# Expert stage: next slot's second unit and two weight pieces moved behind the second layer's first block

## The chip, the cores and the metric

The kernel runs on one core of a Trainium2 chip. The metric is device time in microseconds (us) of one execution, median of the runs. A core has five engines that run side by side: TensorE (PE in the profile; PEld is its loading of stationary operands), VectorE (DVE), ScalarE (ACT), GpSimd (POOL) and SyncE (SP). Semaphores order them. Each engine takes its instructions in the order in which the program issues them.

## The reference

Three parts follow each other, all in float32:

```python
x = attention(q, k, v)                 # 8 x 8 heads, 576 positions, blocks of 64
x = ((x @ w1) * (x @ w2) @ w3) @ w_out # 4608 tokens, 512 -> 1024 -> 512
# mixture of 8 experts, one expert for each token
logits = x @ w_gate                    # (4608, 8)
expert = argmax(logits); gate = softmax(logits)[expert]
for e in range(8):
    out[expert == e] = gate * (relu(x[expert == e] @ e1[e]) @ e2[e])   # 512 -> 1024 -> 512
```

The change touches only the last loop.

## The kernel before

The experts' work is cut into slots. A slot belongs to one expert and holds one unit of 128 token rows (a single) or two (a pair). The order is planned at build time: 17 pairs, with four singles put between them, after the 3rd, 6th, 10th and 13th pair. More singles can follow under a run-time condition; in this run none does. The expert of a slot is known at run time only. GpSimd gathers its weight tables by index: `wload(2 * s)` brings the first layer's table of slot s (128 partitions x 4096 numbers) into raw buffer 0, `wload(2 * s + 1)` the second layer's into raw buffer 1. If the expert is that of the slot before, the index lies out of bounds, and nothing is fetched.

Every matrix product is done in three matmuls, of high and low parts: a float32 operand is split into a rounded high part and the rest. `wsplit(i, c)` splits piece c (1024 of the 4096 columns) of table i: ScalarE copies the high part at L725, and the low part is a subtraction at L727, on GpSimd for piece 1 and on VectorE for the pieces 0, 2 and 3. Three sets of split tables (`wset`) rotate.

`xprep(s, parts)` prepares the rows of a slot: `tr8` transposes each unit by four TensorE transposes (L775) into one of three PSUM scratch buffers, ScalarE copies the high part (L777) and VectorE subtracts for the low part (L778). The buffer is free again after that.

`run` goes through the slots in order: `l1(s)`, then the preparation of the next slot, then `l2(s)`. Nothing reorders the instructions afterwards; what is written between two groups of matmuls is what each engine does between them. `hook1` and `hook2` are called at set points of the two layers and do work for later slots:

- `hook1(0)`: gather the rows of slot s + 2 and split pieces 0 and 1 of table 2s + 2 (the next slot's first layer).
- `hook1(1)`: split pieces 2 and 3 of it, and gather table 2s + 4 into the raw buffer that is free then (the first layer two slots on).
- `hook1(2)`: scatter the last finished output unit to memory.
- `hook2(0)`, `hook2(1)`: split the four pieces of table 2s + 3 (the next slot's second layer), then gather table 2s + 5.

In a pair, `l1` works with the weights as stationary operand, in four parts `f2` of 24 matmuls, each followed by a relu (L832), a subtraction (L833) and a hook. Part f2 needs piece f2 of the split table. In a single, the rows are stationary (L847): two halves of 12 matmuls, each with a relu into `hr` (L850). The hidden rows must then be transposed: `turn(0)` and `turn(1)` do so for each half with `tr8`, which ends in the two halves of `hh` (high) and `hw` (low). The order of a single's `l1` is: first half, relu, `hook(0)` and `hook(1)`, second half, relu, `turn(0)`, the next slot's first unit (`xprep(s + 1, (0,))`), `turn(1)`, `hook(2)`. In `run`, the next slot's second unit follows (`xprep(s + 1, (1,))`).

`l2` sums eight blocks g of three matmuls (L872) for each unit. In block g the first two matmuls read `hh[:, g]`, the third `hw[:, g]`; blocks 0 to 3 need only what `turn(0)` wrote. Behind blocks 1 and 3 come `hook2(0)` and `hook2(1)`. At the end ScalarE scales and copies the output (L878).

Of the kernel before, what the change touches and what calls it, by code (L numbers as in the profile page):

```python
# [31 lines left out]
def slot_order(nt):  # L32

    npr, nsg = slots(nt)
    now = min(nsg, 4)
    order = []
    for j in range(npr):
        order.append((True, j))
        for m in range(now):
            if j == (m + 1) * npr // (now + 1) - 1:  # L40
                order.append((False, m))
    order += [(False, m) for m in range(nsg) if (False, m) not in order]
    return order, npr + now
# [3 lines left out]
def tile_moe_stack(ctx: ExitStack, tc: tile.TileContext, qd, kd, vd, w1, w2, w3t, wo, wg,  # L47
# [10 lines left out]
    order, NOW = slot_order(NT)  # L58
# [671 lines left out]
    def units(s):  # L730
        pair, j = order[s]
        return (s, NSL + j) if pair else (s,)
# [7 lines left out]
    def experts(sc):  # L740
# [9 lines left out]
        def scatter():  # L750
            if ys:
                un, y = ys.pop(0)
                nc.gpsimd.indirect_dma_start(  # L753
                    out=out, out_offset=bass.IndirectOffsetOnAxis(ap=ids[:, un:un + 1], axis=0),
                    in_=y[:], in_offset=None, bounds_check=NT - 1, oob_is_err=False)
# [8 lines left out]
        def rload(s):  # L764
            rows[s] = []
            for h in range(len(units(s))):
                x = gx.tile([128, RW], F32, tag=f"x{h}", name=f"x{h}")
                rgather(s, h, 1, x[:])
                rows[s].append(x)

        def tr8(src, dh, dl):
            for h, (s_, o_) in enumerate(src):
                ps = ps_t.tile([128, 512], F32, tag="t", name="t")
                for c in range(4):
                    nc.tensor.transpose(ps[:, 128 * c:128 * c + 128], s_[:, 128 * c:128 * c + 128], ident)  # L775
                ps = ps.rearrange("p (k c) -> p k c", c=128)
                nc.scalar.activation(out=o_(dh), in_=ps, func=AF.Copy)  # L777
                nc.vector.tensor_tensor(out=o_(dl), in0=ps, in1=o_(dh).bitcast(F32), op=ALU.subtract)  # L778

        def xprep(s, parts=(0, 1)):  # L780
            o_ = 256 * (s % 2)
            xh, xl = xhl[:, 0:4, o_:o_ + 256], xhl[:, 4:8, o_:o_ + 256]
            tr8([(x, lambda t, h=h: t[:, :, 128 * h:128 * h + 128]) for h, x in enumerate(rows[s]) if h in parts], xh, xl)
            xts[s] = (xh, xl)
# [16 lines left out]
        def pair_mm(s, f2, ps, k0, k1):  # L801
            xh, xl = xts[s]
            wh_, wl_ = (w_.rearrange("p (c k n) -> p c k n", c=4, k=4) for w_ in wset[2 * s % 3])
            for d in range(2):
                for k_ in range(k0, k1):
                    for c, (u, x) in enumerate(((wh_, xh), (wh_, xl), (wl_, xh))):
                        nc.tensor.matmul(ps[:, d], lhsT=u[:, f2, k_, 128 * d:128 * d + 128],  # L807
                                         rhs=x[:, k_], start=(k_ == 0 and c == 0 and (s > 0 or d == 0)),
                                         stop=(k_ == 3 and c == 2 and (s > 0 or d == 1)))
# [10 lines left out]
        def l1(s, hook, more):  # L820
            xh, xl = xts[s]
            wh_, wl_ = (w_.rearrange("p (c k n) -> p c k n", c=4, k=4) for w_ in wset[2 * s % 3])
            if order[s][0]:
                for f2 in range(4):
                    if s == 0:
                        ps = first[f2]
                        pair_mm(s, f2, ps, 2, 4)
                    else:
                        ps = ps_h.tile([128, 2, 256], F32, tag="h", name="hps")
                        pair_mm(s, f2, ps, 0, 4)  # L830
                    o_ = slice(2 * f2, 2 * f2 + 2)
                    nc.scalar.activation(out=hh[:, o_], in_=ps, func=AF.Relu)  # L832
                    nc.vector.scalar_tensor_tensor(out=hw[:, o_], in0=ps, scalar=0.0, in1=hh.bitcast(F32)[:, o_],  # L833
                                                   op0=ALU.max, op1=ALU.subtract)
                    hook(f2)
            else:
                hr = hp.tile([128, 1024], F32, tag="hr", name="hr")

                def turn(i):
                    tr8([(hr[:, 512 * i:512 * i + 512], lambda t: t[:, 4 * i:4 * i + 4, 0:128])], hh, hw)  # L840

                for f2 in range(2):
                    ps = ps_h.tile([128, 512], F32, tag="h", name="hps")
                    c = 0
                    for k_ in range(4):
                        for x, u in ((xh, wh_), (xl, wh_), (xh, wl_)):
                            nc.tensor.matmul(ps.rearrange("p (c n) -> p c n", c=2), lhsT=x[:, k_, 0:128],  # L847
                                             rhs=u[:, 2 * f2:2 * f2 + 2, k_], start=(c == 0), stop=(c == 11))
                            c += 1
                    nc.scalar.activation(out=hr[:, 512 * f2:512 * f2 + 512], in_=ps, func=AF.Relu)  # L850
                    if f2 == 0:
                        hook(0)
                        hook(1)
                turn(0)
                if more:
                    xprep(s + 1, (0,))
                turn(1)
                hook(2)
                hook(3)
            xts.pop(s)  # L860

        def l2(s, hook):
            wh_, wl_ = wset[(2 * s + 1) % 3]
            x2 = rows.pop(s)
            us = units(s)
            for h, un in enumerate(us):
                ps = ps_y.tile([128, 512], F32, tag="y", name="yps")
                o_ = slice(128 * h, 128 * h + 128)
                c = 0
                for g in range(8):  # L870
                    for u, w_ in ((hh, wh_), (hh, wl_), (hw, wh_)):
                        nc.tensor.matmul(ps, lhsT=u[:, g, o_], rhs=w_[:, g * 512:g * 512 + 512],  # L872
                                         start=(c == 0), stop=(c == 23))
                        c += 1
                    if h == 0 and g % 2 == 1:
                        hook(g // 2)
                y = yp.tile([128, 512], F32, tag="y", name="y")
                nc.scalar.activation(out=y, in_=ps, func=AF.Copy, scale=x2[h][:, 512:513])  # L878
                ys.append((un, y))
                if h + 1 < len(us):  # L880
                    scatter()

        def run(s0, s1):
            if s0 == 0:
                rload(0)
                wload(1)
                rload(1)
                l1_begin()
                xhalf(2)
            else:  # L890
                wload(2 * s0 + 1)
                rload(s0)
                for c in range(4):
                    wsplit(2 * s0, c, True)
                xprep(s0)
            if s0 + 1 < s1:
                wload(2 * s0 + 2)
            for s in range(s0, s1):
                last = s + 1 == s1

                def ahead(i):
                    if i < 2 * s1:
                        wload(i)

                def hook1(c):
                    if not last and c < 2:
                        if c == 0 and s + 2 < s1:
                            rload(s + 2)
                        for c_ in (2 * c, 2 * c + 1):
                            wsplit(2 * s + 2, c_)  # L910
                        if c == 1:
                            ahead(2 * s + 4)
                    if c == 2:
                        scatter()

                def hook2(c):
                    if not last and c < 2:
                        for c_ in (2 * c, 2 * c + 1):
                            wsplit(2 * s + 3, c_)
                        if c == 1:  # L920
                            ahead(2 * s + 5)

                if s == s0:
                    for c in range(4):
                        wsplit(2 * s0 + 1, c, True)
                    ahead(2 * s0 + 3)
                l1(s, hook1, not last)
                if not last:
                    xprep(s + 1, (0, 1) if order[s][0] else (1,))
                l2(s, hook2)  # L930
            scatter()

        run(0, NOW)
# [259 lines left out]
```

## Time and profile before

| what | value |
|---|---|
| median of 3 runs | 1570.16 us (1567.07 to 1573.70) |
| profiled execution | 1575.13 us |
| its span, first to last instruction | 1573.40 us |
| mean granted TensorE clock | 0.98 of full speed |
| PE busy | 1510.3 us (96%) |
| DVE busy | 953.4 us (61%) |
| ACT busy | 884.3 us (56%) |
| POOL busy | 732.8 us (47%) |

Busy shares are averages over the whole program. PE counts as busy while a matmul is in its pipeline, also at a lowered clock. [...] The expert stage is the last part of the span, from about 1080 us. In a timeline row the first number is the start in us, the second the length of the merged instructions, and a bracket tells how long the engine sat idle before, and what ended that.

### The profile page before, as it was taken

What the parts mean: (1) busy time and instruction counts of PE and PEld (TensorE: products, weight loads), DVE (VectorE), ACT (ScalarE), POOL (GpSimd) and SP (SyncE); (2) the same over time, 40 slices, a digit from 0 to 9 for tenths busy, and PEclk for the clock granted to TensorE, in tenths of its full rate; (3) what the DMA queues carried; (4) which work ended last, traced back from release to release, by engine and by line L of the source; (5) the groups of instructions that cost most, each with busy time, mean ns of one, the idle gap of its engine ahead of it and who ended that gap; (6) DMA issues with size and microseconds to landing.
All of it is one profiled execution on the core that took longest, in us unless ns stands there. A gap on an engine that the chain in (4) does not pass through costs nothing. (4 is left out here: it accounts for less than half of the span.)

```text
span 1573.4 us, 28845 instructions
## 1 busy us (share of the span) xinstructions
PE 1510.3 (96%) x10623; PEld 1416.1 (90%) x10623; DVE 953.4 (61%) x2543; ACT 884.3 (56%) x1959; POOL 732.8 (47%) x727
## 2 busy tenths in 40 slices
PE   6987999999999999999999999998999999999998
PEld 3577999999999999999999999998879889798797
DVE  6689766666666666666469333355755566555652
ACT  4685877676767667676334333332655556454552
POOL 4576766656565565664134111102544454444441
PEclk9699999999999999999999999998999999999999
DMA  5333332232233323320466366545234612545510
GB/s 167 108 123 112 109 102 98 87 103 89 92 99 91 110 87 103 89 87 32 138 170 201 87 169 175 136 126 188 88 104 141 252 51 81 214 144 211 190 41 29
DMA packets 61429, 189.74 MB, mean 121 GB/s; under 512 B 9505, under 2 KB 14498, under 8 KB 58468
## 3 DMA queue, kind: packets, MB, share of 16 engines
q1 hardware_dynamic: 49060, 122.01, 25.8%
q0 software_dynamic: 12224, 65.84, 11.9%
q8 instruction: 86, 1.41, 0.4%
q14 instruction: 59, 0.48, 0.1%
HBM read 187.26 MB, written 43.01 MB: 146 GB/s over the span
## 5 line engine op out<-in xcount | busy, mean ns | idle before, releaser
L304 POOL TENSOR_SCALAR P<-P,m 128x512 f32<-128x512 f32 (+4 forms) x288 | 161.2, 560 | 193.2 <-DVE m L303 124.5
L727 DVE TENSOR_TENSOR wl<-wr,wh 128x1024 fp32r<-128x1024 f32 x128 | 195.8, 1558 | 61.8 <-ACT wh L725 60.8
L872 PE MATMUL yps<-wh,hhw 128*128 128x512 f32 x608 | 201.3, 407 | 1.1 <-DVE hhw L833 1.0
L807 PE MATMUL hps<-xhl,wh 128*128 128x256 f32 x1088 | 198.2, 284 | 2.6 <-ACT xhl L796 2.1
L289 DVE CUSTOM_DVE_ANT_0 P<-s,msk 128x512 f32<-128x512 f32 (+2 forms) x320 | 151.8, 482 | 78.3 <-PE t L321 54.5
L308 DVE TENSOR_TENSOR ptl<-t,pth 128x512 fp32r<-128x512 f32 (+3 forms) x288 | 146.3, 508 | 58.6 <-ACT pth L307 54.6
L297 ACT ACTIVATE P<-P,m 128x512 f32<-128x512 f32 (+4 forms) x288 | 166.9, 579 | 17.3 <-DVE m L289 9.6
L807 PEld LDWEIGHTS hps<-xhl,wh 128*128 128x128 f32 x1088 | 171.1, 191 | 5.2 <-ACT xhl L796 2.7
L725 ACT ACTIVATE wh<-wr 128x1024 fp32r<-128x1024 f32 x168 | 165.5, 1056 | 7.2 <-DMA wr<-e,widx 7.2
L549 PE MATMUL x<-wfh,abh 128*128 128x264 f32 (+1 forms) x576 | 163.8, 284 | 0.0
L549 PE MATMUL x<-wfl,abh 128*128 128x264 f32 (+1 forms) x576 | 162.8, 283 | 0.0
L549 PE MATMUL x<-wfh,abl 128*128 128x264 f32 (+1 forms) x576 | 162.5, 282 | 0.0
L807 PE MATMUL hps<-xhl,wl 128*128 128x256 f32 x544 | 154.8, 285 | 0.0
L872 PEld LDWEIGHTS yps<-wh,hhw 128*128 128x128 f32 x608 | 117.8, 194 | 29.5 <-DVE hhw L833 2.4
L321 PE MATMUL t<-ident,P 128*128 128x128 f32 x768 | 135.4, 279 | 8.4 <-DVE m L302 8.4
L727 POOL TENSOR_TENSOR wl<-wr,wh 128x1024 fp32r<-128x1024 f32 x40 | 99.6, 2490 | 87.5 <-ACT wh L725 87.4
L457 ACT ACTIVATE ab<-mm 128x288 f32<-128x288 f32 x128 | 52.6, 411 | 155.4 <-PE mm L451 154.7
L307 ACT ACTIVATE pth<-t 128x512 fp32r<-128x512 f32 (+3 forms) x288 | 129.2, 448 | 5.0 <-PE t L321 1.8
L351 PE MATMUL av<-pth,VV 128*128 128x256 f32 (+1 forms) x448 | 127.7, 303 | 0.7 <-ACT pth L307 0.7
L351 PE MATMUL av<-ptl,VV 128*128 128x256 f32 (+1 forms) x448 | 125.8, 303 | 2.5 <-DVE m L302 2.2
L833 DVE SCALAR_TENSOR_TENSOR hhw<-hps,hhw 128x512 fp32r<-128x512 f32 x68 | 46.6, 687 | 133.5 <-ACT hhw L832 126.8
L872 PE MATMUL yps<-wl,hhw 128*128 128x512 f32 x304 | 122.6, 403 | 0.0
(231 smaller groups left out, 4429.1 us busy)
## 6 DMA issues: line engine op xcount, KB each, us to landing
qr<-qd SPq DMA_DIRECT2D x29, 640.0 KB, 4.3
abT<-ab SPq DMA_DIRECT2D x64, 288.0 KB, 4.5
abr<-abT SPq DMA_DIRECT2D x36, 512.0 KB, 9.1
kr<-kd SPq DMA_DIRECT2D x29, 576.0 KB, 3.7
vr<-vd SPq DMA_DIRECT2D x32, 320.0 KB, 2.9
str<-w SPq DMA_DIRECT2D x16, 512.0 KB, 4.3
str<-w3t SPq DMA_DIRECT2D x16, 512.0 KB, 3.6
x2d<-row SPq DMA_DIRECT2D x7, 1026.0 KB, 9.1
```

The lines of the kernel that those rows point to most:

```text
L289: nc.vector.tensor_tensor_reduce(out=pr[:, o_:o_ + w_], in0=s_, in1=msk[:, c_:c_ + w_], scale=-0.125, scalar=BIG, op0=ALU.add, op1=ALU.min ...
L297: nc.scalar.activation(out=pr, in_=pr, func=AF.Exp, bias=m[:, 0:1], scale=-1.0, accum_out=m[:, 3:4])
L304: nc.gpsimd.tensor_scalar(out=pr, in0=pr, scalar1=m[:, 6:7], scalar2=1.0, op0=ALU.mult, op1=ALU.mult)
L307: nc.scalar.activation(out=dst_h, in_=src, func=AF.Copy)
L308: nc.vector.tensor_tensor(out=dst_l, in0=src, in1=dst_h.bitcast(F32), op=ALU.subtract)
L321: nc.tensor.transpose(t_[:, 128 * c:128 * c + 128], pr[:, 128 * c:128 * c + 128], ident)
L351: nc.tensor.matmul(t_[:, x0:n], lhsT=vv[:, k_, hd, :], rhs=pt[:, hd, o_ + x0:o_ + n], start=(c == 0), stop=(c == 2 * kcs - 1))
L549: nc.tensor.matmul(ps[:, :c1 - c0], lhsT=u[:, k_, j * 128:j * 128 + 128], rhs=w_[:, k_, c0:c1], start=(c == 0), stop=(c == 23))
L725: nc.scalar.activation(out=h_[:, sl], in_=rawt[i % 2][:, sl], func=AF.Copy)
L727: (nc.gpsimd if c == 1 and not pre else nc.vector).tensor_tensor(out=l_[:, sl], in0=rawt[i % 2][:, sl], in1=h_[:, sl].bitcast(F32), op=ALU ...
L807: nc.tensor.matmul(ps[:, d], lhsT=u[:, f2, k_, 128 * d:128 * d + 128], rhs=x[:, k_], start=(k_ == 0 and c == 0 and (s > 0 or d == 0)), sto ...
L872: nc.tensor.matmul(ps, lhsT=u[:, g, o_], rhs=w_[:, g * 512:g * 512 + 512], start=(c == 0), stop=(c == 23))
```

## The change

In a single slot, four things move from the first layer, or from between the layers, to a new point `begun` behind block 0 of the second layer: the transposes and splits of the next slot's second unit, the split of pieces 2 and 3 of table 2s + 2 with the gather of table 2s + 4 behind it, and the scatter. Pairs keep their order. (`hook(3)` did nothing.)

```diff
                     if f2 == 0:
                         hook(0)
-                        hook(1)
                 turn(0)
                 if more:
                     xprep(s + 1, (0,))
                 turn(1)
-                hook(2)
-                hook(3)
             xts.pop(s)
 
-        def l2(s, hook):
+        def l2(s, hook, begun):
...
                         c += 1
+                    if h == 0 and g == 0:
+                        begun()
                     if h == 0 and g % 2 == 1:
                         hook(g // 2)
...
                 l1(s, hook1, not last)
-                if not last:
-                    xprep(s + 1, (0, 1) if order[s][0] else (1,))
-                l2(s, hook2)
+                if not last and order[s][0]:
+                    xprep(s + 1, (0, 1))
+
+                def begun():
+                    if not order[s][0]:
+                        if not last:
+                            xprep(s + 1, (1,))
+                        hook1(1)
+                        hook1(2)
+
+                l2(s, hook2, begun)
```

## Rows read from the trace of the kernel before

**Rows 1.** List of waits of PE, whole span: waited for, us in total, times, longest.

```profile
PE t L775 <- DVE hhw L778: 9.3, 4, 2.3
...
PE t L775 <- ACT hr L850: 5.2, 4, 1.3
...
PE yps L872 <- DVE hhw L833: 1.0, 1, 1.0
```

**Rows 2.** Windows of three singles, a pair, and the first single's second layer.

```profile
core 0: us, PE busy (x) PEld busy (x) DVE busy (x) ACT busy (x) POOL busy (x), PEclk, DMA share, GB/s
1165.17:1183.67 18.50, 14.89 (x65) 11.82 (x64) 12.18 (x10) 11.40 (x15) 8.73 (x6) 0.91 0.17 50
...
1364.94:1384.57 19.63, 16.02 (x65) 12.79 (x64) 12.51 (x10) 11.39 (x15) 8.69 (x6) 0.83 0.36 140
1454.23:1473.61 19.38, 15.77 (x66) 12.60 (x64) 12.51 (x10) 11.39 (x15) 8.78 (x6) 0.82 0.68 256
1183.67:1207.05 23.38, 23.38 (x154) 21.25 (x152) 13.36 (x13) 12.32 (x16) 12.12 (x10) 1.00 0.43 136
1176.45:1183.67 7.22, 7.22 (x27) 5.73 (x26) 6.12 (x6) 4.38 (x5) 4.24 (x3) 0.76 0.06 18
```

**Rows 3.** Timeline of PE between the layers of the first single.

```profile
1170.74 0.60 PE L775 MATMUL t<-ident,hr 128*128 128x128 f32 x4
1171.17 0.60 PE L775 MATMUL t<-ident,x 128*128 128x128 f32 x4
1173.07 0.66 PE L775 MATMUL t<-ident,hr 128*128 128x128 f32 x4 [1.30 <-ACT hr L850]
1176.04 0.66 PE L775 MATMUL t<-ident,x 128*128 128x128 f32 x4 [2.32 <-DVE hhw L778]
```

**Rows 4.** Timeline of PE between the layers of the pair behind it.

```profile
1195.04 1.03 PE L775 MATMUL t<-ident,x 128*128 128x128 f32 x8
1195.83 0.48 PE L872 MATMUL yps<-wh,hhw 128*128 128x512 f32 x1
```

**Rows 5.** Timeline of ACT in the first single.

```profile
1168.64 3.89 ACT L725 ACTIVATE wh<-wr 128x1024 fp32r<-128x1024 f32 x4
1172.43 0.58 ACT L850 ACTIVATE hr<-hps 128x512 f32<-128x512 f32 x1
1172.91 0.60 ACT L777 ACTIVATE hhw<-t 128x512 fp32r<-128x512 f32 x1
```

**Rows 6.** Timeline of DVE in the first single and in the pair behind it.

```profile
1169.72 1.23 DVE L727 TENSOR_TENSOR wl<-wr,wh 128x1024 fp32r<-128x1024 f32 x1 [8.14 <-ACT wh L725]
1171.62 3.77 DVE L727 TENSOR_TENSOR wl<-wr,wh 128x1024 fp32r<-128x1024 f32 x2 [0.67 <-ACT wh L725]
1175.31 0.68 DVE L778 TENSOR_TENSOR hhw<-t,hhw 128x512 fp32r<-128x512 f32 x1
...
1190.20 0.69 DVE L833 SCALAR_TENSOR_TENSOR hhw<-hps,hhw 128x512 fp32r<-128x512 f32 x1 [0.67 <-ACT hhw L832]
...
1195.87 0.69 DVE L833 SCALAR_TENSOR_TENSOR hhw<-hps,hhw 128x512 fp32r<-128x512 f32 x1 [1.25 <-ACT hhw L832]
```

**Rows 7.** Timeline of POOL: first single, the pair behind it, last single.

```profile
1170.73 2.44 POOL L727 TENSOR_TENSOR wl<-wr,wh 128x1024 fp32r<-128x1024 f32 x1 [3.48 <-ACT wh L725]
...
1189.30 2.50 POOL L727 TENSOR_TENSOR wl<-wr,wh 128x1024 fp32r<-128x1024 f32 x1 [0.96 <-ACT wh L725]
...
1465.23 1.02 POOL L716 DMA_INDIRECT wr<-e,widx  x1 [3.00 <-DVE hhw L778]
```

**Rows 8.** Windows behind the gather of table 2s + 4, second and last single.

```profile
1265.00:1271.00 6.00, 6.00 (x21) 4.74 (x20) 4.89 (x5) 4.28 (x5) 3.84 (x3) 0.72 0.03 6
...
1466.00:1474.00 8.00, 8.00 (x30) 6.41 (x29) 5.97 (x5) 4.57 (x6) 3.76 (x3) 0.72 0.84 298
```

**Rows 9.** Timeline of ACT in the first slot.

```profile
1099.89 3.90 ACT L725 ACTIVATE wh<-wr 128x1024 fp32r<-128x1024 f32 x4 [3.06 <-DMA wr<-e,widx]
```

**Rows 10.** Timeline of PE at the start of the stage, and a window behind it.

```profile
1096.88 0.38 PE L807 MATMUL hps<-xhl,wh 128*128 128x256 f32 x1 [1.42 <-ACT xhl L796]
...
1098.00:1099.00 1.00, 1.00 (x8) 1.00 (x8) 0.00 (x0) 0.00 (x0) 0.00 (x0) 0.69 0.83 324
```

## The prediction

> **What bounds the kernel now.** I read first, on the page, the busy shares: TensorE leads all engines throughout, so a time is lost where it waits or where its clock is low. The list of its waits then names the places. In the expert stage, two waits stand out: four of 2.3 us for the VectorE subtraction at L778 and four of 1.3 us for the ScalarE copy at L850 [rows 1]. Four is the number of single slots in the planned order. The windows of these slots show the rest: 18.50, 18.50 (the slot at 1253.33 reads as the one at 1165.17), 19.63 and 19.38 us, 76.01 in all, at mean clocks of 0.91, 0.91, 0.83 and 0.82, while the pair slot behind the first one is fully busy at clock 1.00 [rows 2]. So pairs are bound by TensorE, and only singles lose.
>
> What would a single cost without loss? Its 24 first-layer matmuls take 5.57 us (1165.17 to 1170.74), four transposes 0.43 us, so sixteen 1.72 [rows 2, 3]. In the pair, 48 second-layer matmuls take 11.22 us (1195.83 to 1207.05), so 24 take 5.61 [rows 2, 4]. That is 12.90 us a single, 51.6 for four. The loss is 76.01 - 51.6 = 24.4 us. By the starts on TensorE, the third group of transposes starts 1.47 us late (1171.60 to 1173.07) and the fourth 2.54 (1173.50 to 1176.04) [rows 3]; four times 4.01 is 16.0 us. The other 8.4 us are low clock behind the waits: the first single's second layer takes 7.22 us at clock 0.76 where 5.61 is enough [rows 2].
>
> **Where the two waits come from.** ScalarE runs the first relu, then four weight copies from 1168.64 for 3.89 us, and only then the second relu, at 1172.43, although its matmuls end about 0.2 us behind the start of the next work at 1170.74 (my estimate from 0.4 us matmuls that start 0.23 apart) [rows 3, 5]. VectorE runs the subtraction of piece 0 at 1169.72, those of pieces 2 and 3 for 3.77 us from 1171.62, and only at 1175.31 the first hidden half's subtraction [rows 6]. The transpose scratch has three PSUM buffers, and the fourth group reuses the first one's, so it waits for that subtraction.
>
> **What the change removes.** Pieces 2 and 3 (two ScalarE copies, two VectorE subtractions) go behind the first block of the second layer. ScalarE is then free of pieces 0 and 1 at about 1168.64 + 1.95 = 1170.6, before the second half is computed; the second relu starts at about 1170.95 and ends at 1171.55, when TensorE has just finished the next slot's first unit (1171.60). The first wait goes. The relu's successors start 0.48 apart [rows 5], so the first hidden half is copied from 1171.4 to 1172.0. VectorE is free at 1170.95 and subtracts it from 1172.05 to 1172.73 (0.68) [rows 6]. The second wait goes too: the moved transposes now need the buffer behind the first block, after 1172.73.
>
> **What is new on TensorE.** Twelve transposes end their issue at 1172.05. The first block is three matmuls; the first two need only the copy, the third the subtraction done at 1172.73. Issued without a wait it would start at 1172.52, so I charge 0.25 us a single, 1.0 in all. The bounds are 0 and 1.9 us a single: the latter if the block waited for the second half's subtraction too (about 1173.95). I take the low one, since the pair's second layer starts at 1195.83, before the last hidden subtraction starts at 1195.87, so it waits by part, not by whole tile [rows 4, 6]. GpSimd subtracts piece 1 for 2.44 us from 1170.73, at the same time as these subtractions [rows 7]. If it held them all back until 1173.17, 1.1 us would be lost. But in the pair L833, which like them reads PSUM, takes 0.69 us at 1190.20 inside a GpSimd subtraction from 1189.30 [rows 6, 7]; price 0. The moved transposes cost what they cost before, 0.43 us.
>
> **What moves on the other engines.** Counted from the single's start, the next slot begins at about 13.15 us. ScalarE does the moved unit's copy at 8.4, pieces 2 and 3 until 10.9, the next four pieces until 14.7 and the output copy until 15.3; its next relu comes at 16.0. VectorE ends piece 3 at 12.4 and the next table's at about 16.2. The pair wants piece 2 at 13.15 + 2 x 2.85 = 18.9 (its first layer runs in four parts of 2.85, from 1183.67 to 1195.04) [rows 2, 4], so 6 us are to spare. If that cover were gone, each late us would be a TensorE us.
>
> No line that the change touches issues on SyncE's queue. GpSimd's keeps its order, but the gather of the weights two slots on, then the scatter of the previous slot, now stand behind piece 3: issued at 13.2 instead of 11.0 us. Behind them wait the next piece-1 subtraction (done by 18.3, wanted in the second layer at 26.8) and the next gather. Who waits for this one is ScalarE, which wants its data at 17.0. In three singles nothing is fetched, because the expert repeats: 6 GB/s in the 6 us behind the issue [rows 8]. In the last one the load runs: issued at 1465.23, it and a scatter move 2.4 MB by 1474.0, so it lands 8.8 us behind its issue [rows 7, 8]. After the change that is at 22.0, and ScalarE stands 5 us with relus queued behind it. TensorE goes on through the first layer (three PSUM buffers); the second layer starts at 25.4 and its third quarter's subtraction, pushed behind the late pieces, comes about 1 us late. The nearest row is the first slot, where ScalarE waits 3.06 us for such a load and TensorE then 1.0 us for L833 [rows 1, 9]. I charge 1.0 us, once; bounds 0 and 5.
>
> **Sum.** 24.4 - 1.0 - 1.0 = 22.4 us. The profiled execution took 1575.13 us (span 1573.40 and 1.73 around it), so 1552.7 by its own time. It is 5.0 us above the median of three, 1570.16; the median becomes 1547.8, I say 1548.
>
> **The clock.** The sum takes it that the 8.4 us of low clock go with the waits. What the rows bear out: 8 transposes in a row (0.79 us) leave the pair at clock 1.00 [rows 2, 4]. [...] After the change the stretch between first and second layer has 1.3 us of transposes and 0.25 us of waiting, with TensorE never idle longer than that. [...]
>
> [...]
>
> **Rivals.**
> 1. The clock falls anyway in all four singles: 8.4 us stay, 22.4 - 8.4 = 14.0 gained, 1556. For it: the fall at 1098. Against: hardly any idle time is left. 0.15.
> 2. The wait moves into the first block, which waits for both halves: 1.9 instead of 0.25, so 6.6 us less, 1554. Against: the pair's partial wait. 0.06.
> 3. The late gather stalls TensorE for the full 5 us: 1552. Against: the first slot's row. 0.03.
> 4. The change does not do what it says, because pieces 2 and 3 and the moved unit reach the pair so late that its first layer waits for what the single gained. It would need VectorE 6 us later than I place it, and 4 to 5.6 us more at all four, which takes back 16 to 22 us: 1564 to 1570. Against: VectorE is busy 12 to 12.5 us in a single now, so 13 us are nearly full but still enough [rows 2]. 0.05.
> 5. Slower: the clock falls in each single and stays at the half level into the next pair. Each us there costs half a us. Today's second layer spends 2 x (1 - 0.76) x 7.22 = 3.5 us at that level [rows 2]. The waits give 14.0 us net, so another 28 us, 7 a single, at half level would cancel them, and about 11 a single would make the kernel 0.5% slower (7.9 us): 1578 or more. Against: the pair behind each single now runs at full clock. 0.03.
>
> The forecast itself has 0.68. 1543 is the low end: all 24.4 us, and 3.1 us as the lowest of the three runs lies under the median. The high end is rival 1 with 1 us for the runs' spread, 1557; rivals 2 and 3 lie inside. Half a per cent, 7.9 us, is about what a measurement of this kernel can tell from no change. The forecast and rivals 1 to 3 are faster than that: 0.92. Rival 4 is same: 0.05. Rival 5 is slower: 0.03.
>
> **What the profile after would show.** The two waits at L775 gone from the list; ScalarE's two copies, not four, between the relus; single windows of about 13.2 us, the last one's following pair about 1 us longer; the clock at 1.00 in the second layers; one short wait of the first block for L778; the gather two slots on issued behind the single's end. I am wrong if the single keeps a clock below 1.00, if L872 shows waits of over 1 us for L778, or if a pair behind a single is longer than 23.4 us at more than one place.

## The result and the profile after

The changed kernel takes 1546.74 us (median of 5 runs, 1545.98 to 1554.69) against 1570.16 us; the ratio is 0.9855, with a 95% interval of 0.9831 to 0.9878. Forecast were 1548 us and a range of 1543 to 1557. The profiled execution of the changed kernel took 1554.69 us (span 1552.9, against 1573.4 before). Lines behind L853 have other numbers now: L872 of before is L869.

The windows of the four singles, and of the pair behind the last one (first column the stretch, then its length, the engines' busy time, the clock, DMA):

```profile
core 0: us, PE busy (x) PEld busy (x) DVE busy (x) ACT busy (x) POOL busy (x), PEclk, DMA share, GB/s
1166.87:1180.16 13.29, 13.29 (x65) 10.63 (x64) 6.91 (x8) 9.92 (x14) 4.22 (x3) 1.00 0.20 59
1249.81:1263.09 13.28, 13.28 (x65) 10.63 (x64) 6.90 (x8) 9.91 (x14) 4.28 (x3) 1.00 0.50 198
1356.17:1369.45 13.28, 13.28 (x65) 10.63 (x64) 6.90 (x8) 9.91 (x14) 4.23 (x3) 1.00 0.50 199
1439.13:1452.41 13.28, 13.28 (x65) 10.62 (x64) 6.89 (x8) 9.91 (x14) 4.25 (x3) 1.00 0.50 199
1452.41:1476.52 24.11, 23.66 (x153) 21.18 (x152) 16.72 (x15) 13.58 (x18) 15.02 (x10) 1.00 0.56 218
```

They answer to [rows 2]: 53.13 us for four singles instead of 76.01, all at clock 1.00, and one pair that is 0.7 us longer than the 23.37 of most others. That is a gain of 22.1 us inside the stage; the forecast was 22.4. The spans differ by 20.5, because in this execution the first single begins 1.7 us later (1166.87 against 1165.17), behind work that the change does not touch.

That the median came within 1.3 us of the forecast is chance in part: the same kernel, run again (same_again), had a median of 1551.23 us beside 1567.99 for the kernel before. The windows above are the firmer answer.

The list of waits of PE in the expert stage, to be held against [rows 1]: both waits at L775 are gone. Of the three waits for L833, two (1.06 and 0.42 us) stand in the first slot, where the change does nothing; the third, 0.45 us, is the late gather's, shown below. The short wait of the first block for L778, which the forecast named, is not in the list; it shows in the starts alone.

```profile
PE t L793 <- DMA msk<-x2b,ids: 2.7, 2, 2.2
PE hps L807 <- ACT xhl L796: 2.1, 2, 1.4
PE yps L869 <- DVE hhw L833: 1.9, 3, 1.1
PE hps L807 <- DVE xhl L797: 0.3, 1, 0.3
```

PE between the layers of the first single, where [rows 3] stood:

```profile
1172.44 0.60 PE L775 MATMUL t<-ident,hr 128*128 128x128 f32 x4
1172.87 0.60 PE L775 MATMUL t<-ident,x 128*128 128x128 f32 x4
1173.31 0.64 PE L775 MATMUL t<-ident,hr 128*128 128x128 f32 x4
1173.78 0.50 PE L869 MATMUL yps<-wh,hhw 128*128 128x512 f32 x1
1174.11 0.40 PE L869 MATMUL yps<-wl,hhw 128*128 128x512 f32 x1
1174.50 0.51 PE L869 MATMUL yps<-wh,hhw 128*128 128x512 f32 x1
1174.85 0.60 PE L775 MATMUL t<-ident,x 128*128 128x128 f32 x4
```

The three transpose groups now follow each other by 0.43 to 0.47 us, the first block comes at once, and only its third matmul is held, by about 0.16 us. ACT and DVE in the same single ([rows 5, 6] before), in one fence each:

```profile
1170.34 2.00 ACT L725 ACTIVATE wh<-wr 128x1024 fp32r<-128x1024 f32 x2
1172.63 0.60 ACT L850 ACTIVATE hr<-hps 128x512 f32<-128x512 f32 x1 [0.29 <-PE hps L847]
1173.13 0.59 ACT L777 ACTIVATE hhw<-t 128x512 fp32r<-128x512 f32 x1
...
1461.07 2.01 ACT L725 ACTIVATE wh<-wr 128x1024 fp32r<-128x1024 f32 x2 [5.00 <-DMA wr<-e,widx]
```

```profile
1173.76 0.69 DVE L778 TENSOR_TENSOR hhw<-t,hhw 128x512 fp32r<-128x512 f32 x1 [1.10 <-ACT hhw L777]
```

ACT waits for the matmuls of the second half instead of the matmuls waiting for ACT, and DVE idles 1.1 us before the subtraction that used to come last in its queue. The last ACT row is the price: in the pair behind the last single ACT stands 5.00 us for the late gather. The gather's issue on GpSimd, and what the wait comes to on TensorE, in the third quarter of the pair's second layer:

```profile
1452.47 1.25 POOL L716 DMA_INDIRECT wr<-e,widx  x1 [5.31 <-DVE wl L727]
```

```profile
1468.52 0.73 PE L869 MATMUL yps<-wh,hhw 128*128 128x512 f32 x2 [0.45 <-DVE hhw L833]
```

### The profile page after: what moved, and what is told of

The parts are those of the page before. It is cut to its first block, busy times and chain, and to the rows that moved or that the text cites. A ratio compares the mean times of both kernels' runs of the same rounds, so it can differ in the third digit from the quotient of the medians.

```text
span 1552.9 us, 28837 instructions
## 1 busy us (share of the span) xinstructions
PE 1504.0 (97%) x10623; PEld 1410.4 (91%) x10623; DVE 947.3 (61%) x2543; ACT 885.0 (57%) x1959; POOL 742.6 (48%) x727
## 5 line engine op out<-in xcount | busy, mean ns | idle before, releaser
L727 DVE TENSOR_TENSOR wl<-wr,wh 128x1024 fp32r<-128x1024 f32 x128 | 189.1, 1510 | 62.8 <-ACT wh L725 56.5
L869 PE MATMUL yps<-wh,hhw 128*128 128x512 f32 x608 | 197.4, 399 | 2.0 <-DVE hhw L833 1.9
L869 PEld LDWEIGHTS yps<-wh,hhw 128*128 128x128 f32 x608 | 113.8, 188 | 31.1 <-DVE hhw L833 3.8
L716 POOL DMA_INDIRECT wr<-e,widx x42 | 47.1, 1122 | 152.4 <-DVE wl L727 55.4
L869 PE MATMUL yps<-wl,hhw 128*128 128x512 f32 x304 | 119.6, 394 | 0.0
```

Source lines behind the costliest of these rows:

```text
L727: (nc.gpsimd if c == 1 and not pre else nc.vector).tensor_tensor(out=l_[:, sl], in0=rawt[i % 2][:, sl], in1=h_[:, sl].bitcast(F32), op=ALU ...
```

## The experiments

Each kernel differs from the changed one by the edit shown. A single's time is taken from its first matmul to the next slot's, by the timeline; it repeats to a few hundredths where the clock does not fall, and so tells more than the whole time, whose runs of one kernel spread by 0.4 to 1.3%. Ratios are to the kernel before, run beside each.

| kernel | the four singles, us | pair behind the last, us | ratio, 95% interval |
|---|---|---|---|
| before | 18.50, 18.50, 19.63, 19.38 | 23.36 | 1 |
| changed | 13.29, 13.28, 13.28, 13.28 | 24.11 | 0.9855 (0.9831 to 0.9878) |
| same_again | 13.28, 13.29, 13.28, 13.28 | 24.33 | 0.9886 (0.9854 to 0.9919) |
| pieces_only | 13.68, 13.69, 13.68, 13.71 | 23.50 | 0.9899 (0.9872 to 0.9926) |
| unit_only | 18.11, 16.55, 18.09, 19.04 | 23.37 | 0.9966 (0.9941 to 0.9991) |
| copies_early | 14.75, 14.76, 14.78, 14.79 | 23.93 | 0.9909 (0.9879 to 0.9940) |
| long_transposes | 16.42, 16.42, 16.41, 16.41 | 24.77 | 0.9931 (0.9897 to 0.9965) |
| idle_instead | 16.67, 18.23, 19.15, 19.11 | 23.38 | 1.0017 (0.9992 to 1.0042) |
| begun_late | 13.30, 13.30, 13.29, 13.29 | 27.92 | 0.9888 (0.9849 to 0.9926) |
| hidden_first | 13.07, 13.08, 13.02, 13.07 | 25.09 | 0.9874 (0.9843 to 0.9906) |

**same_again.** No edit.

> The changed kernel itself, beside the others: 13.28 us a single, and a ratio to the kernel before of 0.985 to 0.988. The runs so far differ by some 5 us before the first single begins, where the change does nothing.

The singles repeat to 0.01 us. The ratio, 0.9886, lies just above the forecast 0.985 to 0.988; its interval overlaps the upper half of the first one. "Some 5 us" was too little: in the profiled executions the first single begins between 1157.25 and 1171.86 us (last section).

**pieces_only.** Which of the two moves is it? First the pieces alone:

```diff
-                if not last and order[s][0]:
-                    xprep(s + 1, (0, 1))
+                if not last:
+                    xprep(s + 1, (0, 1) if order[s][0] else (1,))
 
                 def begun():
                     if not order[s][0]:
-                        if not last:
-                            xprep(s + 1, (1,))
                         hook1(1)
                         hook1(2)
```

> The next slot's second unit stays between the layers, as before the change; pieces 2 and 3, the gather and the scatter stay behind the first block. Theory 1 (the gain is the two waits that the pieces caused on ScalarE and VectorE, and the clock that fell behind them): nearly the whole gain is here. The unit's transposes wait about 0.7 us for their PSUM buffer, and the first block then waits no more for the subtraction, so a single takes 0.3 us more than after the change: 1548 us, clock 1.00 in the singles. Theory 2 (moving the unit matters as much, since it brings matmuls earlier behind the transposes): half the gain, about 1558.

A single takes 13.7 us. The only wait of TensorE left there is that of the unit's transposes for their buffer:

```profile
PE t L775 <- DVE hhw L778: 2.2, 4, 0.6
```

The singles gain 76.01 - 54.76 = 21.25 us, where the changed kernel gains 22.88; theory 2, half the gain, is out by that. The whole time alone would have misled: 1548 and 1558 of 1570 are 0.986 and 0.992, and the interval of the measured ratio (0.9872 to 0.9926) holds theory 2's figure and not theory 1's. It also overlaps that of same_again, the changed kernel itself.

**unit_only.** The other half: the unit behind the first block, the pieces back in the first layer.

```diff
                     if f2 == 0:
                         hook(0)
+                        hook(1)
                 turn(0)
...
                 turn(1)
+                hook(2)
             xts.pop(s)
...
                         if not last:
                             xprep(s + 1, (1,))
-                        hook1(1)
-                        hook1(2)
```

> Only the next slot's second unit moves behind the first block; pieces 2 and 3, the gather and the scatter stay in the first layer. Theory 1: the second relu still comes late (1.5 us a single), and the wait for the subtraction moves from the transposes into the first block (about 2.1 instead of 2.5 us), so a single takes 16.4 us at full clock and 18.0 if the clock falls as before: 1559 to 1566 us. Theory 2: half the gain or more, 1558 or less.

The waits are where theory 1 puts them (first single, PE):

```profile
1167.02 0.66 PE L775 MATMUL t<-ident,hr 128*128 128x128 f32 x4 [1.30 <-ACT hr L850]
1169.99 0.50 PE L871 MATMUL yps<-wh,hhw 128*128 128x512 f32 x1 [1.76 <-DVE hhw L778]
```

Its singles, by windows:

```profile
1159.12:1177.23 18.11, 15.05 (x65) 11.84 (x64) 11.25 (x9) 11.40 (x15) 8.75 (x6) 0.91 0.17 51
1246.93:1263.48 16.55, 13.49 (x66) 10.63 (x64) 9.94 (x9) 11.41 (x15) 8.37 (x6) 1.00 0.41 161
1356.59:1374.68 18.09, 15.03 (x66) 11.77 (x64) 11.48 (x10) 11.41 (x15) 8.72 (x6) 0.91 0.39 153
1444.34:1463.38 19.04, 15.98 (x65) 12.56 (x64) 11.72 (x10) 11.40 (x15) 8.79 (x6) 0.82 0.68 255
```

71.8 us for the four: with the unit's move alone they take 4.2 us less, of the 22.9. Of these, 1.9 are the second single, in which the clock, by the same two waits, happened not to fall, and 1.5 the third, whose mean clock was 0.91 instead of 0.83. The first and the last, whose clock is as before, gain 0.4 and 0.3. The wait for L778 is the same wait, now standing in the first block.

**copies_early.** Which of the two waits costs what? ScalarE's copies of pieces 2 and 3 go back, the subtractions stay moved:

```diff
                     if f2 == 0:
                         hook(0)
+                        hook("hi")
...
                 def hook1(c):
+                    if c == "hi":
+                        if not last:
+                            for c_ in (2, 3):
+                                wsplit(2 * s + 2, c_, "hi")
+                        return
...
                         for c_ in (2 * c, 2 * c + 1):
-                            wsplit(2 * s + 2, c_)
+                            wsplit(2 * s + 2, c_, "lo" if c == 1 and not order[s][0] else False)
```

> As after the change, but ScalarE's two copies of pieces 2 and 3 go back into the first layer; VectorE's two subtractions stay behind the first block. This leaves the first wait (second relu late, 1.47 us a single) and takes the second away: 14.7 us a single at full clock, 1552 us. If 1.47 us of idle time in a stretch of 2.8 us without matrix work is enough for the clock to fall, as at the start of the stage, 1.6 us more a single: about 1559. The theory that only the longer wait mattered gives 1547 to 1549.

```profile
1160.64:1175.39 14.75, 13.45 (x65) 10.63 (x64) 7.15 (x9) 11.40 (x15) 4.39 (x4) 1.00 0.18 53
...
1437.38:1452.17 14.79, 13.49 (x65) 10.63 (x64) 7.19 (x9) 11.40 (x15) 4.45 (x4) 1.00 0.45 177
```

```profile
PE t L775 <- ACT hr L850: 5.2, 4, 1.3
```

14.77 us, 1.5 more than the changed kernel: the relu's wait has come back at its full size, and the clock stays at 1.00 in all four. So ScalarE's queue is worth 1.5 x 4 = 6 us of the 22.9. The rest, about 17, goes with VectorE's two subtractions (their wait, and the clock) and, for some 0.4 us a single, with the unit's move. unit_only and copies_early differ in the place of these subtractions and of the gather and scatter behind them; at full clock a single takes 16.55 us in the one and 14.76 in the other, and the difference is the wait of 1.76 us for L778. Whether that wait alone, at this size and without the relu's, would lower the clock was not run: the subtractions need the copies ahead of them.

**long_transposes and idle_instead.** What lowers the clock? The first makes the stretch between the layers long without leaving TensorE idle:

```diff
                 turn(1)
+                dm = ps_h.tile([128, 512], F32, tag="h", name="dm")
+                for r in range(32):
+                    q_ = 128 * (r % 4)
+                    nc.tensor.transpose(dm[:, q_:q_ + 128], hr[:, q_:q_ + 128], ident)
             xts.pop(s)
```

> As after the change, with 32 more transposes of the hidden rows between the layers of each single, into a PSUM buffer that nobody reads: the stretch without matrix work is 4.8 us, but TensorE is never idle in it. If idle time lowers the clock: it stays at 1.00, and the run costs 4 x 3.46 us less the short wait of the first block, 1559 us. [...]

The second adds no work to TensorE, but lets it idle:

```diff
                             wsplit(2 * s + 2, c_)
+                        if c == 0 and not order[s][0]:
+                            for r in range(2):
+                                wsplit(2 * s + 2, 0, "lo")
```

> As after the change, but VectorE repeats the subtraction of piece 0 twice (the same result) before the hidden halves, so that the first block's third matmul waits about 3.2 us: 16.2 us a single at full clock, nearly as long as with the 32 transposes. If idle time of TensorE lowers the clock and transposes do not, the clock falls here in most singles though the stretch without matrix work is no longer than there, 1.6 to 2.4 us more for each: 17.8 to 18.6 us a single, 1565 us in all. If the stretch must hold both waits, as before the change, it stays at 1.00: 1559.

First and last single with the transposes (the two between read the same, at clock 1.00), and the long group in one of them (L860):

```profile
1171.86:1188.28 16.42, 16.42 (x97) 14.16 (x96) 6.89 (x8) 9.92 (x14) 4.24 (x3) 1.00 0.16 49
...
1453.57:1469.98 16.41, 16.41 (x97) 14.15 (x96) 6.89 (x8) 9.91 (x14) 4.23 (x3) 1.00 0.41 161
```

```profile
1177.87 0.60 PE L775 MATMUL t<-ident,x 128*128 128x128 f32 x4
1178.31 0.64 PE L775 MATMUL t<-ident,hr 128*128 128x128 f32 x4
1178.78 3.66 PE L860 MATMUL dm<-ident,hr 128*128 128x128 f32 x32
1182.19 0.48 PE L873 MATMUL yps<-wh,hhw 128*128 128x512 f32 x1
```

The four singles with the idle time, and the wait in one of them:

```profile
1157.65:1174.32 16.67, 13.30 (x66) 10.62 (x64) 11.32 (x10) 9.93 (x14) 4.20 (x3) 1.00 0.16 47
1243.96:1262.19 18.23, 14.86 (x65) 11.86 (x64) 12.49 (x11) 11.39 (x15) 5.50 (x4) 0.91 0.36 143
1355.31:1374.46 19.15, 15.78 (x65) 12.54 (x64) 12.81 (x11) 11.53 (x15) 5.63 (x5) 0.82 0.35 138
1444.13:1463.24 19.11, 15.74 (x65) 12.50 (x64) 12.77 (x11) 11.52 (x15) 5.63 (x5) 0.82 0.35 139
```

```profile
1168.66 0.51 PE L869 MATMUL yps<-wh,hhw 128*128 128x512 f32 x1 [3.37 <-DVE hhw L778]
```

VectorE's three subtractions ahead of that one, in the same single:

```profile
1162.20 5.80 DVE L727 TENSOR_TENSOR wl<-wr,wh 128x1024 fp32r<-128x1024 f32 x3 [8.17 <-ACT wh L725]
```

With 44 transposes in a row, 4.8 us (1177.43 to 1182.19) and no matrix work, the clock stays at 1.00 in all four. With 3.37 us idle, behind the usual three groups of transposes and two matmuls, it falls in three of four, and the first single shows what the wait costs without the fall (16.67). Over the kernels, 3.06 to 3.62 us of idle time between the layers went with a mean clock of 0.82 to 0.91 in ten of twelve singles (before four, unit_only three, idle_instead three), the transposes in none of four. So the low clock goes with idle time here, not with the kind of work. idle_instead also shows VectorE's queue as the cause of the wait, since beside the changed kernel it moves no copy, no gather and no scatter. Its last two singles, 19.15 and 19.11 us, took longer than the forecast 17.8 to 18.6. Its whole time came out worse than forecast, 1571.9 against 1565: its singles alone say 2.9 us less than before, and its runs spread from 1564 to 1583, at mean clocks of 0.989 and 0.974. Where the rest comes from is open.

**begun_late.** How much cover does the late gather have? All that `begun` does moves on to behind block 3, and so behind `hook2(0)`, the first two pieces of the next slot's second layer:

```diff
-                    if h == 0 and g == 0:
+                    if h == 0 and g == 3:
                         begun()
```

> The moved work is done behind block 3 of the second layer instead of block 0. Theory 1 (a late gather costs TensorE about what it comes later, once the slack is used up): the singles stay at 13.0 to 13.3 us; the gather two slots on is issued 2 to 3 us later, ScalarE waits 7 to 8 us for it in the pair behind the last single, and that pair takes 26 to 27 us instead of 24.1; the other pairs 23.4. Rival (the transfer is hidden anyway): that pair stays at 24.1. Rival 4 of the prediction (the pieces reach the pair late): all four pairs behind singles get longer by 1 us or more.

The pair behind the last single, the gather, and ScalarE's wait:

```profile
1452.08:1480.00 27.92, 25.66 (x153) 22.18 (x152) 17.53 (x16) 13.77 (x18) 13.48 (x11) 0.94 0.49 189
```

```profile
1454.20 1.25 POOL L716 DMA_INDIRECT wr<-e,widx  x1 [3.12 <-DVE wl L727]
```

```profile
1462.97 2.01 ACT L725 ACTIVATE wh<-wr 128x1024 fp32r<-128x1024 f32 x2 [7.24 <-DMA wr<-e,widx]
```

The gather comes 15.4 us into the single instead of 13.3, and the pair takes 3.8 us more than in the changed kernel, and 4.55 more than 23.37: 27.92 - 25.66 = 2.3 us of waiting and 25.66 - 23.37 = 2.3 us, most of it from the lowered clock (0.94 over 27.92 us, which I estimate at 0.06 x 27.92 = 1.7 us), which the forecast (26 to 27) had not counted. The pairs behind the other three singles, where nothing is fetched, keep 23.4 us. So the transfer is not hidden anyway, and the pieces do not reach the pair too late: the rival and rival 4 are out.

The cover itself can be read across the runs. ScalarE waits for this gather 3.45 us in idle_instead, 4.41 in pieces_only, 4.83 in copies_early, 5.00 in the changed kernel, 5.23 in same_again, 5.64 in long_transposes and 5.99 in hidden_first, and the pair there is 0.0, 0.13, 0.56, 0.74, 0.96, 1.40 and 1.72 us longer than 23.37. So the first 4.3 us of the wait cost TensorE nothing, and each us beyond costs about one, as far as 5.99 us; at 7.24 us (begun_late) the clock falls too, to a mean of 0.94 over the pair.

**hidden_first.** Does covering the last short wait help?

```diff
+                todo = [(g, t) for g in range(8) for t in range(3)]
+                if len(us) == 1:
+                    todo = [(0, 0), (0, 1), (1, 0), (1, 1), (0, 2), (1, 2)] + todo[6:]
                 for g in range(8):
-                    for u, w_ in ((hh, wh_), (hh, wl_), (hw, wh_)):
+                    for g_, t in todo[3 * g:3 * g + 3]:
+                        u, w_ = ((hh, wh_), (hh, wl_), (hw, wh_))[t]
...
-                    if h == 0 and g == 0:
+                    if h == 0 and g == 1:
```

> As after the change, but in a single the second layer begins with the four matmuls of blocks 0 and 1 that read the high parts, then the two that read the low parts, and the moved work follows. The wait for the first subtraction is covered: 12.9 to 13.0 us a single instead of 13.28, and the gather is issued 0.5 us later, which costs up to 0.5 us behind the last single. About 1 us in all, less than the runs can tell.

The singles get 0.2 us shorter each, 0.9 in all (13.02 to 13.08, where 12.9 to 13.0 was forecast); the pair behind the last one gets 1.0 longer (25.09), twice the forecast's most, since the gather is issued 13.76 us into the single instead of 13.33 and ScalarE waits 5.99 us for it. Nothing is left over, and the interval overlaps that of the changed kernel. No version here is shown to beat the change.

## Why the prediction was right, step by step

- **Size and place of the loss** (24.4 us: 16.0 in two waits, 8.4 in the clock behind them). Confirmed: with both gone the singles take 53.13 us, 22.9 less. Each cause was shown on its own: the relu behind four copies by copies_early (1.5 us a single, 1.47 read), the subtraction behind three others by the pair unit_only and copies_early (1.76 us at full clock) and by idle_instead. That the low clock goes with idle time is shown by idle_instead (3.37 us idle, a clock of 0.82 to 0.91 in three singles of four) against long_transposes (4.8 us of transposes, 1.00 in all four); how the 8.4 us of it divide between the two waits is not shown.
- **The new wait in the first block** (0.25 us a single). A single takes 13.28 us, 0.38 over the 12.90 without loss, so 1.5 us in all instead of 1.0. So this term was 0.13 us a single too small. Part of it is the wait (0.16 by the starts in the first single; hidden_first, which covers it, gains 0.2), the rest lies, by the starts in the first single, around the two switches between transposes and matmuls: the second matmul behind a switch starts 0.33 (1173.78 to 1174.11) and 0.32 us (1175.20 to 1175.52) after the first, and the moved transposes 0.35 (1174.50 to 1174.85) after the matmul ahead of them, where 0.23 is the spacing elsewhere; they themselves take 0.35 instead of 0.43. Bounds and choice held: subtraction and block do meet by part, as the pair's row had said. Rival 2 did not come.
- **GpSimd beside the subtractions** (0). L778 took 0.69 us at 1173.76 inside GpSimd's subtraction from 1172.43, as L833 had:

```profile
1172.43 2.47 POOL L727 TENSOR_TENSOR wl<-wr,wh 128x1024 fp32r<-128x1024 f32 x1 [3.50 <-ACT wh L725]
```

- **The late gather** (1.0 us once, bounds 0 and 5). The issue was forecast at 13.2 us into the single and came at 13.3; ScalarE waited 5.00 us, as forecast; TensorE lost 0.7 us, at the place that was named (the third quarter's subtraction, 0.45 us of idle time at 1468.52), and without the move (unit_only) the pair has its 23.37. The forecast gave the wait 4 us of cover, the runs 4.3. begun_late shows what lies beyond: 2.1 us more cost 3.8. Rival 3 did not come. With the block's 0.5 us more and this 0.3 us less, the two charges came to 2.2 us instead of 2.0, so that two misses cancel in part.
- **The clock** stayed at 1.00; rival 1 did not come. For it stood the fall at 1098, behind 1.42 us of idle time: by half microseconds the clock of the kernel before reads 1.00 from 1097.5, 0.87 from 1098.0 and 0.50 from 1098.5. This 0.50 is the half level of rival 5. The first single before was at it too, from 1177 to 1180; with 0.89 in the 0.55 us ahead and 0.85 in the 1 us behind, that is about 3.4 us, where rival 5 has 3.5. Rival 5 did not come either: the pairs behind the four singles are at 1.00. 44 transposes in a row (long_transposes, 4.8 us) leave the clock at 1.00, four times of four; whether they would raise a lowered clock no run shows. What the low clock goes with at this place is idle time: 3.37 us a single in idle_instead, and 0.91, 0.82 and 0.82 in three of four.
- **Which move does it** the prediction had not separated. pieces_only has 21.25 of the 22.88 us in the singles, unit_only 4.2, of which some 3 come from a clock that fell in fewer places; the moves share the clock, so the two do not add up. The unit's move is worth having for 0.4 us a single: it takes its transposes out of the wait for a buffer.

## What to carry to other kernels

A wait of TensorE is to be priced with the clock that is read behind it: here 16.0 us of waiting went with 8.4 us more in slow matmuls, while the 5.2 us of waiting in copies_early, at clock 1.00, went with none. Work for later slots belongs behind the point where an engine has handed over what TensorE waits for: four copies made the next relu 1.5 us late, two left ScalarE idle for 0.29 us before it. What is moved back takes its followers along; the one to check is the transfer that can only start behind it, and the traffic behind each issue shows whether it fetches anything.

## What the runs showed that was not expected

- Whether the clock falls is not fixed by the waits alone: in unit_only it fell behind the same 1.30 and 1.76 us of idle time in three singles and not in the fourth, and in idle_instead behind 3.37 us in three of four. Behind 1.30 us between transposes (copies_early) it fell in none of four. What decides is open.
- Much of the spread of the whole time arises early. In the first 110 us, in attention, the mean clock was 0.97 in one execution and 0.83 in another, and the first single began at 1159.10 and at 1171.86 us, in kernels that do not differ there (same_again, long_transposes). Over the ten profiled executions the first matmul with w1 (L451, the layer that runs beside attention) came between 101.3 and 115.2 us, and the first single 1055.0 to 1057.6 us after it. Whether the low clock causes the delay or only goes with it is not shown.

```profile
0.00:110.00 110.00, 88.24 (x396) 60.91 (x397) 84.29 (x278) 77.03 (x195) 69.20 (x86) 0.97 0.47 142
```

```profile
0.00:110.00 110.00, 89.28 (x312) 57.94 (x313) 74.40 (x247) 67.71 (x170) 61.93 (x77) 0.83 0.41 122
```

- The gather behind the first single, whose indices are all out of bounds, was not free for its reader. From 1180 to 1184 the DMA engines moved 29 GB/s, 0.12 MB (from 1453 to 1461, behind the gather that loads, 303 GB/s); yet it was issued at 1180.20, and ScalarE could use the buffer at 1183.99, having waited 0.18 us for it:

```profile
1183.99 2.01 ACT L725 ACTIVATE wh<-wr 128x1024 fp32r<-128x1024 f32 x2 [0.18 <-DMA wr<-e,widx]
```
